# Strassen scheme: the second product a quarter unit later, casts in 2 KB rows, one quadrant cast by ScalarE, w_in's split stored

## The chip, the cores and the metric

The kernel runs on one core of a Trainium2 chip. The metric is the device time of one execution in microseconds, as the median of several runs. Beside it there is one profiled execution, whose trace gives each instruction with its start, its length and what it waited for.

## The reference

Two stages follow each other. Channel attention over 4 batches of 6080 tokens with 256 channels, then a feed-forward layer over all 24320 tokens with 2048 hidden channels:

```python
def _attn_ref(q, k, v, tau):                    # q, k, v: (4, 6080, 256) float32
    qn = q / (np.linalg.norm(q, axis=1, keepdims=True) + 1e-06)
    kn = k / (np.linalg.norm(k, axis=1, keepdims=True) + 1e-06)
    s = kn.transpose(0, 2, 1) @ qn / tau        # (4, 256, 256)
    a = np.exp(s - s.max(-1, keepdims=True))
    a /= a.sum(-1, keepdims=True) + 1e-09
    return v @ a

def _moe_ref(x, w_in, w_out):                   # x: (24320, 256), w_in: (256, 2048), w_out: (2048, 256)
    h = x @ w_in
    g = np.where(h > 0.0, h, np.exp(np.minimum(h, 0.0)) - 1.0)
    return g @ w_out
```

## The kernel before

**What is multiplied.** Attention's result is not formed: `a` is folded into the weights, so that the first product of a batch is `v` times (`a` times `w_in`), the second is `g @ w_out`. Each float32 operand is split into two parts, a high part rounded to TensorE's fast type (float32r) and a low part, the rest. A product is then three matmuls: high by high, high by low, low by high. "hi" and "lo" in names are these parts; a *cast* makes a high part, a subtraction on VectorE the low part.

**Stages.** The first 596 us hold batch 0 and the preparation of batch 1. Then comes the Strassen stage: batches 1 to 3 in 36 chunks of 512 or 496 tokens, each chunk in 4 *units* (`fq`, 512 hidden channels each), 144 units in all. Beside the units of batches 1 and 2 TensorE, and the others, compute the next batch's attention: 24 row groups of q and k each (gram matmuls, lines 203 and 210; squares for the norms), then the norms and the softmax, then the next weights (`plan_s`).

**A unit's first product.** The 2x2 blocks of weights and tokens are multiplied by the Strassen-Winograd scheme: seven `product` calls of six matmuls each (line 1102), into three PSUM banks. `A11 B11` goes into `bank_a`, `S3 T3` into `bank_e`; ScalarE copies them to `bank_b` and to the SBUF tile `p7`; `S2 T2`, `S1 T1` and `S4 B22` add into `bank_b`, `A12 B21` into `bank_a`, `A22 T4` into `bank_e`, and VectorE makes the sums between them (lines 1490 and 1498). The four quadrants of h then stand in `bank_a` (e11), `bank_b` (e12), `bank_e` (e21) and `p7` (e22). `relu_exp` (ScalarE, two instructions) and `largest` (VectorE) turn each into g, in the tile `held`.

**Splitting g.** `hi_part` casts one quadrant by a DMA that GpSimd issues (line 1186); `lo_parts` subtracts for a row of two quadrants (line 1189). Row 0 is e11 and e12 (tile `g1`), row 1 is e21 and e22 (`g2`). The last cast (e21) and both low parts are issued in the next unit: the cast behind `A11 B11`, row 0's low part ahead of VectorE's sum after `S2 T2`, row 1's behind that sum.

**The second product.** A unit gives eight *items* to the list `outs` (four 128-channel pieces of g by two halves of the output); an item is three matmuls (lines 1125 to 1127) into the accumulators `po`. `multiply_out(n, now)` takes n items off the list at fixed places between the products: 2, 1, 2, 1 and 2 a unit. With 6 items of the stage before and four empty entries at its head, the list runs 10 items behind: row 0's first item stands behind the next unit's `A12 B21`, and row 1's last two behind the second product of the unit after it.

**What sets the order.** On the five engines the order is the order in which Python issues instructions. The work for later batches is in queues of tasks, one per engine and level. A unit is 4 ticks; `spend(engine, budget, now)` takes tasks that are ready at tick `now` off an engine's queues, lower levels first, while their listed costs fit the budget. A task is ready when its `when` has come and each task that it depends on was issued at least `GAP` (or `late`) ticks ago. Between matmuls of the items, `beside` issues matmuls of the PE queue. A square (ScalarE, line 1287) writes the only buffer `sq`; GpSimd then issues a DMA that adds `sq` to `acc` (line 1290), and the next square waits until that has landed.

## Time and profile before

| | |
|---|---|
| median of 2 runs | 2329.24 us (2328.5 to 2329.99) |
| profiled execution | 2332.99 us, span 2331.2 us, mean granted TensorE clock 0.977 |
| busy share of the span | TensorE 94%, VectorE 69%, ScalarE 61%, GpSimd 27% |
| DMA | 345.47 MB; GpSimd's queue 38.9% of 16 engines, SyncE's 15.9% |
| the Strassen stage | begins 596 us after the span's start |

A row of a timeline gives the start in us from the span's start, the length in us, the engine, the line and operation, output<-inputs, and in brackets the idle time ahead of it with what ended it. A row of a group ends in busy us, mean ns of one, idle us before them and what ended most of that. A row of stretches gives for each engine the busy us with the number of instructions, then the granted TensorE clock as a share of full speed, the mean busy share of the DMA engines, and GB/s. A row of DMA issues gives the number, the size of one, and the median us from issue to landing. PE is TensorE, PEld its weight loads, DVE VectorE, ACT ScalarE, POOL GpSimd, SP SyncE.

### The profile page before, as it was taken

To read this page: it belongs to the slowest core of one execution; us is meant where nothing else is said; L and a number is where in the kernel's file an instruction comes from. 1 tells how busy PE (TensorE), PEld (TensorE's weight loads), DVE (VectorE), ACT (ScalarE), POOL (GpSimd) and SP (SyncE) were. 2 spreads that over 40 slices of the span, in tenths; PEclk is the share of its full clock that TensorE was granted. 3 is DMA by queue.
4 is the path that set the end of the run, shared out by engine and by line. 5 is a ranking of instruction groups with operands and counts; after the bars stand their busy time and mean duration, and the time that the engine had idled before them with its cause. 6 is when DMAs were issued, how large, how long until landed. Compare 5 with 4: busy or idle time off the path is not lost. (4 is left out here: it accounts for less than half of the span.)

```text
span 2331.2 us, 35484 instructions
## 1 busy us (share of the span) xinstructions
PE 2200.9 (94%) x12833; PEld 1967.5 (84%) x12833; DVE 1599.7 (69%) x2322; ACT 1419.1 (61%) x2380; POOL 633.4 (27%) x909
## 2 busy tenths in 40 slices
PE   9999999999898898899998898898899999999999
PEld 8888888998787777788997787787798889988988
DVE  7987777778665565567676666665677667767765
ACT  6877676677555455556565555555566566666665
POOL 0000000001333333332444333343334433333332
PEclk9999999999999999999999999999999999999999
DMA  9221222211577877675567777787557545555543
GB/s 338 93 87 36 79 64 73 66 40 50 148 194 183 208 194 179 174 178 143 152 162 212 198 200 203 183 202 188 147 147 187 152 125 150 138 146 131 144 126 108
DMA packets 264174, 345.47 MB, mean 148 GB/s; under 512 B 19776, under 2 KB 198976, under 8 KB 264000
## 3 DMA queue, kind: packets, MB, share of 16 engines
q0 software_dynamic: 201600, 224.17, 38.9%
q1 hardware_dynamic: 62256, 118.91, 15.9%
q8 instruction: 102, 1.67, 0.3%
q14 instruction: 72, 0.59, 0.1%
q10 hardware_dynamic: 144, 0.13, 0.0%
HBM read 134.33 MB, written 27.00 MB: 69 GB/s over the span
## 5 line engine op out<-in xcount | busy, mean ns | idle before, releaser
L1186 POOL DMA_DIRECT2D g<-held x576 | 409.8, 712 | 1061.1 <-issue 390.0
L1125 PE MATMUL po<-g,wo 128*128 128x512 f32 (+1 forms) x1158 | 453.1, 391 | 74.0 <-DMA g<-held 69.9
L1189 DVE TENSOR_TENSOR g<-held,g 128x1024 fp32r<-128x1024 f32 (+1 forms) x288 | 351.4, 1220 | 242.4 <-DMA g<-held 216.2
L1127 PE MATMUL po<-g,wo 128*128 128x512 f32 (+1 forms) x1158 | 455.8, 394 | 27.7 <-DVE g L1189 27.0
L1126 PE MATMUL po<-g,wo 128*128 128x512 f32 (+1 forms) x1158 | 447.2, 386 | 0.0
L1180 ACT ACTIVATE held<-held 128x512 f32<-128x512 f32 (+1 forms) x576 | 360.6, 626 | 18.3
L1125 PEld LDWEIGHTS po<-g,wo 128*128 128x128 f32 x1158 | 226.6, 196 | 96.3 <-issue 58.2
L1127 PEld LDWEIGHTS po<-g,wo 128*128 128x128 f32 x1158 | 225.4, 195 | 81.9 <-DVE g L1189 52.6
L1102 PEld LDWEIGHTS bank_b<-t,s 128*128 128x128 f32 x1728 | 238.6, 201 | 48.2 <-DVE bank_e L1490 33.6
L1102 PE MATMUL bank_b<-t,s 128*128 128x256 f32 (+1 forms) x1728 | 263.4, 291 | 11.1 <-ACT bank_b L1480 3.2
L1102 PE MATMUL bank_e<-t,s 128*128 128x256 f32 (+1 forms) x1728 | 241.6, 276 | 3.8 <-DVE held L1183 3.7
L1126 PEld LDWEIGHTS po<-g,wo 128*128 128x128 f32 x1158 | 226.7, 196 | 18.7
L1179 ACT ACTIVATE held<-bank_a 128x512 f32<-128x512 f32 (+1 forms) x144 | 84.8, 589 | 241.9 <-PE bank_a L1102 103.2
L1102 PEld LDWEIGHTS bank_e<-t,s 128*128 128x128 f32 x1728 | 217.0, 193 | 5.7 <-PE bank_a L1102 5.7
L1287 ACT ACTIVATE sq<-raw 128x1024 f32<-128x1024 f32 x46 | 48.8, 1060 | 218.0 <-DMA acc<-sq 212.2
L1102 PE MATMUL bank_a<-s,s 128*128 128x256 f32 (+1 forms) x1296 | 179.6, 275 | 0.0
L1102 PEld LDWEIGHTS bank_a<-s,s 128*128 128x128 f32 x1296 | 170.1, 192 | 5.3
L115 DVE TENSOR_TENSOR g<-e,g 128x512 fp32r<-128x512 f32 (+1 forms) x192 | 131.8, 686 | 48.3 <-ACT g L114 46.9
L114 ACT CAST g<-e 128x512 fp32r<-128x512 f32 (+1 forms) x192 | 116.7, 608 | 69.6 <-DVE e L445 37.6
L1183 DVE SCALAR_TENSOR_TENSOR held<-held,bank_a 128x512 f32<-128x512 f32 (+1 forms) x144 | 97.1, 674 | 85.7 <-ACT held L1180 85.7
L1480 ACT COPY bank_b<-bank_a 128x512 f32<-128x512 f32 (+1 forms) x144 | 81.6, 566 | 111.4 <-PE bank_a L1102 89.2
L1179 ACT ACTIVATE held<-p 128x512 f32<-128x512 f32 (+1 forms) x144 | 89.7, 623 | 91.3 <-DVE p L1498 91.3
(221 smaller groups left out, 4266.7 us busy)
## 6 DMA issues: line engine op xcount, KB each, us to landing
g<-held POOLq DMA_DIRECT2D x384, 256.0 KB, 2.5
g<-held POOLq DMA_DIRECT2D x192, 248.0 KB, 2.5
acc<-sq POOLq DMA_DIRECT2D x46, 512.0 KB, 6.6
raw<-in_q_dram SPq DMA_DIRECT2D x76, 256.0 KB, 3.5
raw<-in_k_dram SPq DMA_DIRECT2D x76, 256.0 KB, 4.2
v<-in_v_dram SPq DMA_DIRECT2D x32, 512.0 KB, 4.2
out_dram<-o SPq DMA_DIRECT2D x56, 256.0 KB, 2.7
qk<-in_q_dram POOLq DMA_DIRECT2D x46, 256.0 KB, 6.6
```

Source lines behind the costliest of these rows:

```text
L114: nc.scalar.copy(hi, src)
L115: nc.vector.tensor_sub(lo, src, hi.bitcast(F32))
L1102: nc.tensor.matmul(bank[:, j, 0:hn], w[:, x, js], y, start=(begin and j == 0 and k == 0), stop=(j == 1 and k == 2), skip_group_check=True,)
L1125: yield nc.tensor.matmul(o, wo[:, f, 0, ds], hi, start=begin, stop=False)
L1126: yield nc.tensor.matmul(o, wo[:, f, 1, ds], hi, start=False, stop=False)
L1127: yield nc.tensor.matmul(o, wo[:, f, 0, ds], lo, start=False, stop=end)
L1179: nc.scalar.activation(e, h, AF.Relu, scale=-1.0)
L1180: nc.scalar.activation(e, e, AF.Exp, scale=-1.0)
L1183: nc.vector.scalar_tensor_tensor(e, e, -1.0, h, op0=ALU.add, op1=ALU.max)
L1186: nc.gpsimd.dma_start(g[:, 0, :, half, 0:hn], e)
L1189: nc.vector.tensor_sub(g[:, 1].rearrange("p j r t -> p (j r) t")[:, :, 0:hn], held[:, x].rearrange("p j r t -> p (j r) t")[:, :, 0:hn], g[ ...
L1480: nc.scalar.copy(vb, va)
```

## The change

- The list `outs` gets six empty entries in place of four, and the places of its items become 2 behind `S3 T3`, 2 behind `A12 B21`, 2 behind `S1 T1`, 2 behind `A22 T4`. The two token halves of an output half follow each other.
- The high parts of g get fixed tiles, one for even and one for odd units, the low parts a third; a quadrant is one row of 2 KB per partition (512 elements) where it was two of 1 KB. Row 1 of odd units is held in two tiles of its own (`others`), and its low part is two subtractions. The weights' tiles (`s_tiles`) are laid out the same way, high parts together.
- e12 is cast by ScalarE, right behind the four quadrants' `relu_exp`.
- Row 0's low part stays ahead of the sum behind `S2 T2`; row 1's goes behind `A22 T4`.
- Batch 1 stores the two parts of `w_in` in DRAM (`wi_scr`); batches 2 and 3 load them by one DMA a quarter, without a load, a cast and two subtractions.
- Square, accumulate and other tasks get other levels, delays (`late`) and budgets; the sum of the two rows of `acc` (`fold_sum`) goes from GpSimd to VectorE; row groups are spread over 30 units (`PACE`) by their due times where it was 24.

The diff, cut to its core:

```diff
     w_scr = dram.tile([FQ, P, KT, CH], F32, name="w_scr")
+    wi_scr = dram.tile([FQ, P, 2, KT, CH], F32, name="wi_scr")
...
         split(hl[:, 0], hl[:, 1], src)
+        nc.sync.dma_start(wi_scr[fq], hl.bitcast(F32))
...
-        s_tiles[fq] = work.tile([P, SPARE + 1, 2, HF], F32R, tag="wp", bufs=2 * KT, name=f"s_{fq}")
+        s_tiles[fq] = work.tile([P, 2, SPARE + 1, HF], F32R, tag="wp", bufs=2 * KT, name=f"s_{fq}")
...
-                gap = 0 if d.engine == self.engine else max(GAP[self.engine], self.late)
+                gap = 0 if d.engine == self.engine else GAP[self.engine] if self.late is None else self.late
...
-                if not able or able[0].cost > budget:
+                if not able or able[0].cost > budget + 0.3:
...
-            task(ACT, 0.6, lambda: copy_out(c, dt), level=0)
+            task(ACT, 0.6, lambda: copy_out(c, dt), level=-1)
...
-    outs += [None] * 4
+    outs += [None] * 6
...
-    held = work.tile([P, 2, 2, 2, HF], F32, tag="qk", bufs=3, name="held")
+    held = work.tile([P, 2, 2, 2 * HF], F32, tag="qk", bufs=3, name="held")
+    others = [work.tile([P, 2 * HF], F32, tag="e", bufs=3, name=f"other_{x}") for x in range(2)]
+    parts_of_g = []
...
-    def hi_part(g, half, e, hn):
-        nc.gpsimd.dma_start(g[:, 0, :, half, 0:hn], e)
...
+    def part_of_g(u, row, x):
+        k = 1 if x else 2 * (u % 2)
+        if len(parts_of_g) == k:
+            parts_of_g.append(work.tile([P, 2, 2, 2 * HF], F32R, tag="g", bufs=3, name=f"g_{k}"))
+        return parts_of_g[k][:, row]
+
+    def hi_part(u, row, half, hn, by_act=False):
+        to, e = part_of_g(u, row, 0)[:, half, 0 : 2 * hn], exact(u, row, half, hn)
+        if by_act:
+            nc.scalar.copy(to, e)
+        else:
+            nc.gpsimd.dma_start(to, e)
+
+    def lo_parts(u, row, hn):
+        hi, lo = (part_of_g(u, row, x)[:, :, 0 : 2 * hn] for x in range(2))
+        if row == 1 and u % 2 == 1:
+            for half in range(2):
+                nc.vector.tensor_sub(lo[:, half], exact(u, row, half, hn), hi[:, half].bitcast(F32))
+        else:
+            nc.vector.tensor_sub(lo, held[:, row, :, 0 : 2 * hn], hi.bitcast(F32))
...
-                nc.gpsimd.dma_start(state[b, "wi", fq][:, 0], w_scr[fq])
...
-            wis = [task(DVE, 0.685, lambda jt=jt: wi_lo(jt), [x, y], level=2, late=2) for jt in range(KT)]
+                nc.gpsimd.dma_start(state[b, "wi", fq], wi_scr[fq])
...
-    PACE = PERIOD * 24 / NG
+    PACE = PERIOD * 30 / NG
...
-            s = task(ACT, 1.05, square, [x, *(acc_done if g else [prior.get("pw")])], when=t + 2, level=3)
+            s = task(ACT, 1.05, square, [x, *(acc_done if g else [prior.get("pw")])], when=t + 2, level=2, late=3 if g else 0)
             if g > 0:
-                acc_done = [task(POOL, 0.55, add, [s], level=2)]
+                acc_done = [task(POOL, 0.55, add, [s], level=1, late=1)]
...
-            nc.gpsimd.tensor_add(acc[:, :, 0, :], acc[:, :, 0, :], acc[:, :, 1, :])
+            nc.vector.tensor_add(acc[:, :, 0, :], acc[:, :, 0, :], acc[:, :, 1, :])
...
         multiply_out(2, now)
         spend(POOL, 3.9, now)
-        spend(ACT, 2.2, now)
-        spend(DVE, 2.8, now)
+        spend(ACT, 2.0, now)
+        spend(DVE, 2.4 if u % (FQ * NB) in (0, *range(FQ * NB - FQ, FQ * NB)) else 1.7, now)
+        product(bank_b, c, fq, "S2", "T2")
         if before is not None:
             before[1]()
-        product(bank_b, c, fq, "S2", "T2")
         nc.vector.tensor_add(ve, vb, vp)
+        product(bank_a, c, fq, "A12", "B21")
+        relu_exp(e11, va)
+        multiply_out(2, now)
+        spend(ACT, 0.7, now + 1)
+        product(bank_b, c, fq, "S1", "T1")
+        nc.vector.tensor_add(vp, vb, vp)
+        multiply_out(2, now + 1)
+        largest(e11, va)
+        hi_part(u, 0, 0, hn)
+        spend(POOL, 1.2, now + 1)
+        product(bank_b, c, fq, "S4", "B22")
+        product(bank_e, c, fq, "A22", "T4")
         if before is not None:
             before[2]()
-        product(bank_a, c, fq, "A12", "B21")
-        relu_exp(e11, va)
-        spend(POOL, 0.6, now + 1)
-        multiply_out(1, now)
-        product(bank_b, c, fq, "S1", "T1")
-        nc.vector.tensor_add(vp, vb, vp)
-        largest(e11, va)
...
-        hi_part(g1, 1, e12, hn)
+        hi_part(u, 0, 1, hn, True)
         multiply_out(2, now + 2)
+        spend(DVE, 1.4, now + 2)
+        spend(ACT, 0.4, now + 2)
+        spend(POOL, 3.3, now + 2)
+        spend(SP, 1, now + 2)
...
-        for y, g in ((2, g1), (0, g2)):
-            for j in range(2):
-                for dt in range(DT):
-                    outs.append((c, 4 * fq + y + j, (g, j), dt))
+        for y, row in ((2, 0), (0, 1)):
+            for dt in range(DT):
+                for j in range(2):
+                    outs.append((c, 4 * fq + y + j, ((u, row), j), dt))
```

Where this moves instructions, the built programs show, engine by engine.

TensorE, from `S2 T2` to `S1 T1` of the 100th unit, before and after (`g1` is row 0, `g2` row 1; after the change `g_0` and `g_2` are the high parts of even and odd units, `g_1` the low parts):

```order
L1102 MATMUL bank_b_5084<-t_0_4714,s_3_5088 128x256 x6
L1102 MATMUL bank_a_16045<-s_1_4869,s_3_5088 128x256 x6
L1125 MATMUL po_36_0_15890<-g1_16004,wo_83 128x512
L1126 MATMUL po_36_0_15890<-g1_16004,wo_83 128x512
L1127 MATMUL po_36_0_15890<-g1_16004,wo_83 128x512
L1102 MATMUL bank_b_5084<-t_0_4714,s_3_5088 128x256 x6
```
```order
L1104 MATMUL bank_b_5089<-t_0_4716,s_3_5095 128x256 x6
L1104 MATMUL bank_a_15868<-s_1_4873,s_3_5095 128x256 x6
L1127 MATMUL po_36_1_15760<-g_2_5249,wo_83 128x512
L1128 MATMUL po_36_1_15760<-g_2_5249,wo_83 128x512
L1129 MATMUL po_36_1_15760<-g_1_5223,wo_83 128x512
L1127 MATMUL po_36_1_15760<-g_2_5249,wo_83 128x512
L1128 MATMUL po_36_1_15760<-g_2_5249,wo_83 128x512
L1129 MATMUL po_36_1_15760<-g_1_5223,wo_83 128x512
L1104 MATMUL bank_b_5089<-t_0_4716,s_3_5095 128x256 x6
```

Before, the first item of the previous unit's row 0 stands between them; now the last two items of the unit before that do, and row 0 begins behind `S1 T1`.

GpSimd, in units of batch 1 with a row group beside them, before and after (casts write `g`, the accumulate `acc`, the casts of the next row group `qk`):

```order
L1186 DMA g1_7371<-held_5086 128x2x256
L1186 DMA g2_7399<-held_5086 128x2x256
L1186 DMA g1_7371<-held_5086 128x2x256
L1186 DMA g2_7399<-held_5086 128x2x256
L1290 DMA acc_2_5211<-sq_7338 128x1024
L1306 DMA qk_7449<-in_q_dram 128x512
L1306 DMA qk_7449<-in_k_dram 128x512
```
```order
L1204 DMA g_0_5162<-held_5091 128x512
L1298 DMA acc_2_5213<-sq_7528 128x1024
L1204 DMA g_0_5162<-held_5091 128x512
L1314 DMA qk_7604<-in_q_dram 128x512
L1314 DMA qk_7604<-in_k_dram 128x512
L1204 DMA g_0_5162<-held_5091 128x512
```

Four casts and then the accumulate have become three casts (e11, e22, e21), with the accumulate behind the first and the row group's casts behind the second.

ScalarE, at the boundary of two units of batch 1, before and after (`held<-bank_b` is e12's `relu_exp`, `held<-bank_e` e21's):

```order
L1179 ACTIVATE held_5086<-bank_b_5084 128x2x256
L1180 ACTIVATE held_5086<-held_5086 128x2x256
L1179 ACTIVATE held_5086<-bank_e_7753 128x2x256
L1180 ACTIVATE held_5086<-held_5086 128x2x256
L1480 COPY bank_b_5084<-bank_a_7866 128x512
L1482 COPY p7_5087<-bank_e_7867 128x512
```
```order
L1183 ACTIVATE held_5091<-bank_b_5089 128x512
L1184 ACTIVATE held_5091<-held_5091 128x512
L1183 ACTIVATE held_5091<-bank_e_7273 128x512
L1184 ACTIVATE held_5091<-held_5091 128x512
L1202 CAST g_0_5162<-held_5091 128x512
L1490 COPY bank_b_5089<-bank_a_7381 128x512
L1492 COPY p7_5094<-bank_e_7382 128x512
```

The cast of e12 now stands between e21 and the copy into `bank_b`.

More of the change, by code (lines that the diff above doesn't have):

```diff
@@ L947, in channel_attention_then_elu_ffn @@
     ACT, DVE, POOL, PE, SP = "act", "dve", "pool", "pe", "sp"
-    queues = {(e, level): [] for e in (ACT, DVE, POOL, PE, SP) for level in range(4)}
+    queues = {(e, level): [] for e in (ACT, DVE, POOL, PE, SP) for level in range(-2, 4)}
     GAP = {ACT: 0, DVE: 0, POOL: 2, PE: 2, SP: 0}
@@ L964, in ready, with task @@
             return True
-    def task(engine, cost, fn, deps=(), when=0, level=1, late=0):
+    def task(engine, cost, fn, deps=(), when=0, level=1, late=None):
         t = Task(fn, tuple(d for d in deps if d is not None), when)
@@ L974, in spend @@
     def spend(engine, budget, now):
-        for level in range(4):
+        for level in range(-2, 4):
             queue = queues[engine, level]
@@ L1312, in plan_rows @@
             h = task(*((POOL, 1.1) if n == 2 else (ACT, 1.05)), hi, before if n == 2 else [x, *before], when=t + PACE * g, level=2)
-            los = [task(DVE, 0.685, lambda y=y, lo=lo: lo(y), [h, x], level=2, late=2 if n == 2 else 0) for y in range(2)]
+            los = [task(DVE, 0.685, lambda y=y, lo=lo: lo(y), [h, x], level=2, late=4 if n == 2 else None) for y in range(2)]
             mine = [s, *los]
@@ L1344, in fold_lo @@
             nc.vector.tensor_sub(parts[:, 1], state[b, "acc"][:, :, 0, :], parts[:, 0].bitcast(F32))
-        f = task(POOL, 1.19, fold_sum, adds, level=1)
-        f = task(ACT, 0.61, fold_hi, [f], level=1)
-        folded = task(DVE, 0.685, fold_lo, [f], level=1)
+        f = task(DVE, 0.685, fold_sum, adds, level=0, late=4)
+        f = task(ACT, 0.61, fold_hi, [f], level=0)
+        folded = task(DVE, 0.685, fold_lo, [f], level=0)
         def row_copy(ct):
@@ L1470, in channel_attention_then_elu_ffn @@
         assert (b, fq) in s_ready, (b, fq, u)
-        e11, e12, e21, e22 = (held[:, x, :, half, 0:hn] for x, half in ((0, 0), (0, 1), (1, 0), (1, 1)))
+        e11, e12, e21, e22 = (
+            exact(u, row, half, hn).rearrange("p (j t) -> p j t", j=2) for row in range(2) for half in range(2)
+        )
         vp = p7[:, :, 0:hn]
```

90 lines of the change are left out of this document (35 added, 55 removed).

## The prediction

> **What bounds the kernel now.** I read the page's head first, then busy time by stage, then the waits, then one bad unit in the timeline. TensorE carries the span.
>
> ```profile
> span 2331.2 us, 35484 instructions
> PE 2200.9 (94%) x12833; PEld 1967.5 (84%) x12833; DVE 1599.7 (69%) x2322; ACT 1419.1 (61%) x2380; POOL 633.4 (27%) x909
> ```
>
> No other engine is near its limit, so what can be won is TensorE's 130 us of idle time and what the idling does to its clock. Where does it idle? The next fence holds three stretches of the Strassen stage twice, first all instructions and then those of line 1102 alone (columns: stretch, length, PE busy, PEld busy, then in the first three DVE, ACT and POOL busy; granted clock; DMA share; GB/s). A unit issues 42 matmuls on line 1102, so the count divided by 42 is the number of units.
>
> ```profile
> 596.00:1082.00 486.00, 427.46 (x2562) 378.21 (x2561) 294.15 (x425) 257.59 (x432) 167.25 (x245) 0.94 0.72 183
> 1215.00:1689.00 474.00, 425.21 (x2573) 375.75 (x2572) 297.29 (x427) 256.87 (x429) 178.28 (x255) 0.96 0.75 191
> 1823.00:2278.00 455.00, 445.50 (x2902) 406.26 (x2901) 319.50 (x448) 284.01 (x485) 155.51 (x221) 0.99 0.53 139
> ...
> 596.00:1082.00 486.00, 206.01 (x1512) 195.77 (x1512) 0.94 0.72 183
> 1215.00:1689.00 474.00, 202.80 (x1511) 192.64 (x1510) 0.96 0.75 191
> 1823.00:2278.00 455.00, 237.94 (x1846) 232.84 (x1845) 0.99 0.53 139
> ```
>
> The two **loaded** stretches, where the next batch's gram runs beside the units, hold 36 units each at 13.5 and 13.2 us; the **light** one holds 44 at 10.35 us. The TensorE timeline gives what a unit must take: from one A11·B11 product to the next, undisturbed, 9.87 us, a product 0.67 us. It also gives the price of the gram: two items of the second product take 1.29 us alone (804.43 to 805.72) and 2.28 us with six gram matmuls between them (807.71 to 809.99), so eight of them, one row group, cost 1.32 us.
>
> ```profile
> 2003.82 0.83 PE L1102 MATMUL bank_a<-s,s 128*128 128x256 f32 x6
> 2004.48 0.83 PE L1102 MATMUL bank_e<-t,s 128*128 128x256 f32 x6
> ...
> 2013.69 0.83 PE L1102 MATMUL bank_a<-s,s 128*128 128x256 f32 x6
> ...
> 804.43 0.38 PE L1125 MATMUL po<-g,wo 128*128 128x512 f32 x1
> ...
> 805.72 0.38 PE L1125 MATMUL po<-g,wo 128*128 128x512 f32 x1
> ...
> 807.71 0.38 PE L1125 MATMUL po<-g,wo 128*128 128x512 f32 x1
> ...
> 809.99 0.83 PE L1102 MATMUL bank_b<-t,s 128*128 128x256 f32 x6
> ```
>
> A loaded stretch therefore needs 36 x 9.87 + 24 x 1.32 = 387 us; it takes 486 and 474, so **99 + 87 = 186 us are lost** there. The light one needs 44 x 9.87 = 434 and takes 455: 21 us, 0.48 us a unit. The waits name the cause, and one loaded unit shows the order of events (columns of the first four: who waited for whom, us in total, times, longest).
>
> ```profile
> DVE g L1189 <- DMA g<-held: 216.2, 112, 6.2
> ACT sq L1287 <- DMA acc<-sq: 212.2, 29, 10.1
> PE po L1125 <- DMA g<-held: 69.9, 33, 4.6
> PE po L1127 <- DVE g L1189: 27.0, 43, 3.0
> ```
> ```profile
> 803.11 1.06 ACT L1287 ACTIVATE sq<-raw 128x1024 f32<-128x1024 f32 x1 [5.55 <-DMA acc<-sq]
> 804.08 0.58 ACT L1179 ACTIVATE held<-bank_a 128x512 f32<-128x512 f32 x1
> ...
> 809.08 1.46 POOL L1186 DMA_DIRECT2D g<-held  x2 [0.21 <-issue]
> 810.53 0.94 POOL L1290 DMA_DIRECT2D acc<-sq  x1
> ...
> 815.98 1.22 DVE L1189 TENSOR_TENSOR g<-held,g 128x1024 fp32r<-128x1024 f32 x1 [6.12 <-DMA g<-held]
> ...
> 815.99 0.45 PE L1125 MATMUL po<-g,wo 128*128 128x512 f32 x1 [4.50 <-DMA g<-held]
> ...
> 817.25 0.80 PE L1127 MATMUL po<-g,wo 128*128 128x512 f32 x1
> 817.86 1.65 PE L1102 MATMUL bank_b<-t,s 128*128 128x256 f32 x6
> 819.30 0.62 PE L1125 MATMUL po<-g,wo 128*128 128x512 f32 x1
> ```
>
> ScalarE stands 5.55 us before a square, because the accumulating DMA that reads `sq` has not landed. The four quadrants behind it come out late and together; GpSimd issues the last two casts at 809.08 and the next accumulate right behind. The last cast lands at 816: VectorE's low part has stood 6.12 us for it, TensorE 4.50. Then, from 815.99 to 819.30, come eleven matmuls (four of a full 512 columns at 0.22 us, one gram matmul at 0.11, a product at 0.67) that need 1.64 us; they take 3.31. The clock is cut, which is the granted 0.94 and 0.96 above (0.06 x 486 + 0.04 x 474 = 48 us of the 186).
>
> **The change, part by part.** The prices:
>
> ```profile
> L1189 DVE TENSOR_TENSOR g<-held,g 128x1024 fp32r<-128x1024 f32 (+1 forms) x288 | 351.4, 1220 | 242.4 <-DMA g<-held 216.2
> L115 DVE TENSOR_TENSOR g<-e,g 128x512 fp32r<-128x512 f32 (+1 forms) x192 | 131.8, 686 | 48.3 <-ACT g L114 46.9
> L114 ACT CAST g<-e 128x512 fp32r<-128x512 f32 (+1 forms) x192 | 116.7, 608 | 69.6 <-DVE e L445 37.6
> ...
> g<-held POOLq DMA_DIRECT2D x384, 256.0 KB, 2.5
> ...
> acc<-sq POOLq DMA_DIRECT2D x46, 512.0 KB, 6.6
> ...
> w_scr<-wf SPq DMA_DIRECT2D x4, 512.0 KB, 2.9
> ```
> ```profile
> q0 software_dynamic: 201600, 224.17, 38.9%
> q1 hardware_dynamic: 62256, 118.91, 15.9%
> ```
>
> *A quarter unit later.* Two of a unit's eight items, 1.29 us, move behind their product, and row 1's four items move past the next unit's first two products: 2 x 0.67 + 1.29 = 2.6 us more for casts and low parts. The mean wait of TensorE for a cast is 69.9 / 33 = 2.1 us, so this alone covers the usual wait, not the longest of 4.6. VectorE still writes row 0's low part ahead of the sum that frees `bank_b` for S1·T1, but two items instead of one stand before that product, 0.65 us more room, and VectorE's side work there has a budget of 1.7 in place of 2.8. Row 1's low part goes from ahead of S1·T1 to behind A22·T4; behind it wait two quadrants' maxima (below, the slower rival).
>
> *The accumulate and the square.* In the old order the square stands right behind the accumulate's issue and pays its landing, 212.2 / 29 = 7.3 us at a time. In the new one the accumulate is issued behind the first quadrant's cast, about 9.3 us into an 11.2 us unit (an estimate from the product and item lengths above), and the next square comes 1.9 us into the next unit, behind the two copies of A11·B11 and S3·T3, that is at 13.1. Landing 6.6 us after its issue, it makes ScalarE wait 9.3 + 6.6 - 13.1 = 2.8 us. Square done 5.6 us into the unit, against 5.0 at which the first quadrant's sum is ready: 0.6 us late, and the second quadrant isn't ready before 8. So this wait is hidden; it costs from landings of about 9 us on.
>
> *One quadrant on ScalarE.* 144 x 608 ns = 88 us more ScalarE work (1419 becomes 1507 us, 65%) and 144 of 576 casts fewer on GpSimd's queue. What stands behind the cast is the copy into `bank_b`, for which the next product waits. In a light unit ScalarE idles there:
>
> ```profile
> 2003.18 0.63 ACT L1180 ACTIVATE held<-held 128x512 f32<-128x512 f32 x1
> 2004.68 0.57 ACT L1480 COPY bank_b<-bank_a 128x512 f32<-128x512 f32 x1 [0.88 <-PE bank_a L1102]
> ```
>
> 0.88 us of idle time covers 0.61: cost nothing, and at most (no cover) 88 us.
>
> *2 KB rows.* No row of the page prices the old cast against the new one, only two queues: 38.9% of 16 engines for 201600 packets is 72 ns for a mean of 1.1 KB, 15.9% for 62256 is 95 ns for 1.9 KB. So half as many packets of twice the size cost about two thirds: the casts' share of the DMA engines falls, by the quarter that leaves and by this. Landing 2.5 us gains between 0 and 0.4 us; I take 0. The Trainium skill ("DMA: Bandwidth & Descriptors", sections "Specifications" and "Anatomy of one DMA — SWDGE (gpsimd) path") speaks against this part: rows of 512 B and more already move at line rate, and a GpSimd DMA costs about 2.0 us plus its bytes at 436 GB/s. That makes 2.6 us for 256 KB whatever the rows (an estimate from that page; the trace has 2.5). By it the rows gain nothing, the DMA engines are relieved only by the quarter that leaves, and the time would stand nearer to the upper end below, about 2178.
>
> *w_in's split stored.* Four stores of 1 MB in batch 1: 0 to 4 x 2 x 2.9 = 23 us if something waited for them; nothing but a buffer two uses later does, so 0. Sixteen low parts of 686 ns go from VectorE (11 us); splitting one low part in two on every second unit gives back 72 x (2 x 686 - 1220) = 11 us. VectorE has 31% idle: 0.
>
> **The sum.** Lost in the loaded stretches: 186. Left there afterwards: between 0 and what a light unit loses now, 0.48; I take half, 0.24 x 72 = 17 us, because a part of the light stretch's loss is itself a wait for low parts, which now come earlier than they are needed (that stretch alone, columns as above):
>
> ```profile
> PE po L1127 <- DVE g L1189: 5.4, 6, 2.3
> ```
>
> The light stretch also loses half of its 21. Gain 186 - 17 + 10 = 179 us; the span becomes 2152. The profiled execution took 2332.99 against a median of 2329.24, so 1.8 us lie around its span and the median is 3.7 lower: 2152 + 1.8 - 3.7 = **2150 us**. With nothing left over it is 2122, with 0.48 us a unit left and no gain elsewhere 2178.
>
> **The rivals.** *Half of it stays* (0.14). The accumulate now sits between the casts of one unit, so the second and third cast queue behind its 512 KB; the DMA engines are 72 to 75% busy in the loaded stretches, and shorter units raise that. If half of the 186 us stay: 2331 - 93 - 5 - 2 = 2231. The 38.9% share speaks for it, the 2.6 us of new distance against it. The Trainium skill ("TensorE: Matmul & The Clock Gate", section "Part 1: The HAM clock gate") has the clock halved only after about 3.4 us of idling. By that rule halved waits would not cut the clock at all, and this case would give back the 24 us that I leave in it for the clock: about 2207. The trace agrees so far as it shows the cut behind a gap of 4.50 us.
>
> *The change doesn't do what it says* (0.08): with landings near the 10.1 us that the longest wait shows, ScalarE still stands 9.3 + 10.1 - 13.1 = 6.3 us before a square and remains the pacemaker, and the bunch of late casts only moves with it. A quarter of the 186 us at most, for the quarter unit, is then won, or nothing: 2283 to 2330. Against it stands the median landing of 6.6.
>
> *Slower* (0.04): VectorE's low part of row 1 now stands between two quadrants' maxima, and ScalarE's cast, with the `bank_b` copy behind it, waits for the second of them. The last cast is issued some 1.9 us into the next unit and its low part's turn comes at 8.6. If it lands later than those 6.7 us (casts land in 2.5, the accumulate that may stand ahead in 6.6), the chain VectorE, ScalarE, TensorE stalls in each unit with a row group. It decides from a mean stall of 3.3 us in 54 such units (three of four loaded ones), which eats the 179 us; at 4.7 us, 3 of waiting and the 1.67 that the cut clock cost above, it is 254 us: 2150 + 254 = 2404.
>
> **Chances.** Forecast 0.70, below it (the floor of 2122 is itself a sum of modelled lengths) 0.04. The range 2112 to 2240 takes in the forecast's ends and the half case. A measurement of this kernel can tell about 2% from no change, 2283 to 2376: faster 0.88, within 0.08, slower 0.04.
>
> **What would show it.** The wait of ScalarE's square for the accumulate falls from 212 us below 100, VectorE's for casts from 216 below 60, TensorE's for casts from 70 below 15; the granted clock of the loaded stretches rises to 0.98 or more and their units go from 13.3 to about 11 us. GpSimd's cast count is 432. I am wrong if TensorE still idles more than 60 us after 596, or if `bank_b` products wait for ScalarE.

## The result, and the profile after

The changed kernel takes **2147.41 us** (median of 2 runs, 2145.76 to 2149.07) against 2329.24: a ratio of 0.9219, 95% interval 0.918 to 0.9259. The forecast was 2150. The page's head, its queue row and the landings of the changed kernel:

```profile
span 2147.3 us, 34893 instructions
PE 2114.3 (98%) x12833; PEld 1934.9 (90%) x12833; DVE 1587.0 (74%) x2380; ACT 1485.0 (69%) x2524; POOL 439.8 (20%) x763
...
q0 software_dynamic: 101376, 191.00, 32.6%
...
g<-held POOLq DMA_DIRECT2D x192, 256.0 KB, 2.3
g<-other POOLq DMA_DIRECT2D x96, 256.0 KB, 4.2
acc<-sq POOLq DMA_DIRECT2D x46, 512.0 KB, 4.7
```

TensorE is idle for 33 us of the span instead of 130. The stretches of the Strassen stage, cut at the first product of a unit: the two loaded ones of 36 units, and 47 units of the light one; below, the last alone with line 1104, the product's line now.

```profile
596.88:994.65 397.77, 389.00 (x2557) 360.21 (x2556) 288.03 (x436) 277.90 (x466) 119.79 (x209) 0.99 0.74 200
1127.27:1524.07 396.80, 390.37 (x2576) 362.37 (x2575) 291.98 (x441) 276.82 (x465) 123.49 (x212) 1.00 0.74 201
...
1657.60:2126.20 468.60, 251.72 (x1974) 248.67 (x1974) 1.00 0.38 115
```

The loaded stretches went from 486 and 474 to 398 and 397 us, 11.05 and 11.02 us a unit: 165 of the span's 184 us come from there. The last 47 units, all light, took 484.6 us before (from 1822.58 to 2307.21) and take 468.6 now, 16 us less or 9.97 us a unit instead of 10.31. The clock that was cut to 0.94 and 0.96 is back at 0.99 and 1.00. The waits that answer to those of before (who waited for whom, us in total, times, longest):

```profile
PE bank_b L1104 <- DVE bank_e L1500: 18.6, 32, 1.5
PE gram L203 <- DVE qk L1318: 4.6, 2, 2.3
PE bank_b L1104 <- ACT bank_b L1490: 3.3, 3, 2.0
...
DVE g L1212 <- DMA g<-held: 24.2, 18, 3.4
...
DVE g L1210 <- DMA g<-other: 7.2, 7, 1.9
...
ACT sq L1295 <- DMA acc<-sq: 19.9, 19, 2.3
```

VectorE's waits for casts of g are two rows now, 31 us together. TensorE no longer waits for a cast at all, and the waits for low parts of g (27.0 us before) are gone too. One loaded unit, which begins at 785.25, and a square of the next:

```profile
785.25 0.83 PE L1104 MATMUL bank_a<-s,s 128*128 128x256 f32 x6
...
785.92 0.54 POOL L1204 DMA_DIRECT2D g<-held  x1 [0.17 <-issue]
...
792.92 1.22 DVE L1212 TENSOR_TENSOR g<-held,g 128x1024 fp32r<-128x1024 f32 x1
...
795.25 0.92 POOL L1298 DMA_DIRECT2D acc<-sq  x1
...
800.18 1.06 ACT L1295 ACTIVATE sq<-raw 128x1024 f32<-128x1024 f32 x1 [1.55 <-DMA acc<-sq]
```

The last cast of a unit (e21, 785.92) has 7.0 us until row 1's low part is due at 792.92, which begins without a wait. The accumulate is issued 10.0 us into the unit and has landed when the next square begins 4.93 us later; ScalarE stood 1.55 us.

### The profile page after: what moved, and what is told of

It reads as the page before. It is cut to its first block, busy times and chain, and to the rows that moved or that the text cites. A ratio compares the mean times of both kernels' runs of the same rounds, so it can differ in the third digit from the quotient of the medians.

```text
span 2147.3 us, 34893 instructions
## 1 busy us (share of the span) xinstructions
PE 2114.3 (98%) x12833; PEld 1934.9 (90%) x12833; DVE 1587.0 (74%) x2380; ACT 1485.0 (69%) x2524; POOL 439.8 (20%) x763
## 3 DMA queue, kind: packets, MB, share of 16 engines
q0 software_dynamic: 101376, 191.00, 32.6%
## 5 line engine op out<-in xcount | busy, mean ns | idle before, releaser
L1127 PE MATMUL po<-g,wo 128*128 128x512 f32 (+1 forms) x1158 | 439.5, 380 | 0.0
L1128 PE MATMUL po<-g,wo 128*128 128x512 f32 (+1 forms) x1158 | 437.7, 378 | 0.0
L1129 PE MATMUL po<-g,wo 128*128 128x512 f32 (+1 forms) x1158 | 437.7, 378 | 0.0
L1204 POOL DMA_DIRECT2D g<-held x288 | 154.0, 535 | 946.6 <-DVE held L1187 612.3
L1212 DVE TENSOR_TENSOR g<-held,g 128x1024 fp32r<-128x1024 f32 (+1 forms) x216 | 264.0, 1222 | 24.9 <-DMA g<-held 24.2
L1184 ACT ACTIVATE held<-held 128x512 f32<-128x512 f32 (+1 forms) x432 | 270.4, 626 | 13.8
L1104 PEld LDWEIGHTS bank_b<-t,s 128*128 128x128 f32 x1728 | 233.6, 192 | 50.3 <-DVE bank_e L1500 33.6
L1506 DVE TENSOR_TENSOR p<-bank_b,p 128x512 f32<-128x512 f32 (+1 forms) x144 | 98.8, 686 | 232.8 <-PE bank_b L1104 232.8
L1104 PE MATMUL bank_b<-t,s 128*128 128x256 f32 (+1 forms) x1728 | 244.4, 278 | 22.2 <-DVE bank_e L1500 18.6
L1129 PEld LDWEIGHTS po<-g,wo 128*128 128x128 f32 x1158 | 219.3, 189 | 28.4
L1128 PEld LDWEIGHTS po<-g,wo 128*128 128x128 f32 x1158 | 220.8, 191 | 17.3
L1127 PEld LDWEIGHTS po<-g,wo 128*128 128x128 f32 x1158 | 221.1, 191 | 13.4
L474 PE MATMUL po<-g,wo 128*128 128x512 f32 (+1 forms) x378 | 142.7, 377 | 0.0
L472 PE MATMUL po<-g,wo 128*128 128x512 f32 (+1 forms) x378 | 142.6, 377 | 0.0
L470 PE MATMUL po<-g,wo 128*128 128x512 f32 (+1 forms) x378 | 142.6, 377 | 0.0
```

Source lines behind the costliest of these rows:

```text
L470: nc.tensor.matmul(o, wo[:, f, 0, ds], hi, start=first(c, f), stop=False)
L472: nc.tensor.matmul(o, wo[:, f, 1, ds], hi, start=False, stop=False)
L474: nc.tensor.matmul(o, wo[:, f, 0, ds], lo, start=False, stop=last(c, f))
L1104: nc.tensor.matmul(bank[:, j, 0:hn], w[:, x, js], y, start=(begin and j == 0 and k == 0), stop=(j == 1 and k == 2), skip_group_check=True,)
L1127: yield nc.tensor.matmul(o, wo[:, f, 0, ds], hi, start=begin, stop=False)
L1128: yield nc.tensor.matmul(o, wo[:, f, 1, ds], hi, start=False, stop=False)
```

## The experiments

Two questions: which part of the change brought the 182 us, and are the parts worth the same by themselves? Each part was undone in the changed kernel, and the two strongest were put alone into the kernel of before.

**The quarter unit undone, e1_lag.** The order of the items and the low parts' places stay as changed.

```diff
-    outs += [None] * 6
+    outs += [None] * 4
-        spend(DVE, 2.4 if u % (FQ * NB) in (0, *range(FQ * NB - FQ, FQ * NB)) else 1.7, now)
+        spend(DVE, 2.4 if u % (FQ * NB) in (0, *range(FQ * NB - 3 * FQ, FQ * NB)) else 1.7, now)
```

> The changed kernel with four empty entries in place of six, so the second product a quarter unit earlier; VectorE's larger budget is given to eight more units of each batch. Theory A: with the accumulate out of the way the casts land 2.3 us after their issue and well ahead of their use; TensorE waits for casts and low parts stay under 30 us, 2150 to 2180. Rival B: the quarter unit was what covered the waits, so most of the loss comes back: 2220 or more.

2431.57 us, ratio 1.0449 (1.0432 to 1.0465): within rival B's "2220 or more", but slower than before, which neither side said. Two waits appear that neither the kernel of before nor the changed one has:

```profile
PE po L1129 <- DVE g L1212: 228.3, 48, 10.4
...
DVE tt L1028 <- DMA v<-in_v_dram: 220.3, 30, 11.5
```

Row 1's low part is issued behind `A22 T4`, and with the list two items earlier TensorE wants its product right behind `A22 T4` too. VectorE itself stands before that for a chunk's load of v. Which of the two set the time isn't separated, so this run says only that the six entries and row 1's low part go together.

**The old order of square and accumulate, e2_square.**

```diff
-            s = task(ACT, 1.05, square, [...], when=t + 2, level=2, late=3 if g else 0)
+            s = task(ACT, 1.05, square, [...], when=t + 2, level=3, late=0)
-                acc_done = [task(POOL, 0.55, add, [s], level=1, late=1)]
+                acc_done = [task(POOL, 0.55, add, [s], level=2, late=4)]
```

> The changed kernel with the old order of the accumulate alone: the accumulating DMA is issued one unit after its square, and the next square stands right behind it on ScalarE. Theory A (ScalarE's blocked square was the head of the chain): ScalarE again stands 4.7 us or more before each of 46 squares (some 200 us in all), the quadrants come late and together, and even with the later second product much comes back: 60 to 150 us, so 2205 to 2300. Rival B (what mattered was the distance between the casts and their use: the quarter unit, the cast on ScalarE, the longer rows): ScalarE waits just as long, but TensorE doesn't; 2147 to 2165.

2272.28 us, ratio 0.9765 (0.9747 to 0.9782): 125 us lost. The wait is back at the size that it had before, with a wait of TensorE behind it:

```profile
ACT sq L1295 <- DMA acc<-sq: 208.0, 32, 9.5
...
PE bank_e L1104 <- DVE held L1187: 38.8, 17, 4.2
```

**e12 cast by a DMA again, e3_e12_dma.**

```diff
-        hi_part(u, 0, 1, hn, True)
+        hi_part(u, 0, 1, hn)
```

> The changed kernel with quadrant e12 cast by a DMA on GpSimd's queue again, issued at the unit's end. Theory A: the low part of row 0 then waits for that DMA, about 2 to 4 us after its issue, ahead of the sum that frees bank_b: VectorE's wait for casts goes from 24 us to 100 or more, TensorE's for VectorE from 19 to 40 to 100, 2165 to 2230. Rival: ScalarE's extra 88 us were a cost, and the time falls by up to 10 us.

2250.91 us, ratio 0.9671 (0.9649 to 0.9692): 103 us lost, for the reason that theory A gives and by more than its 2165 to 2230.

```profile
DVE g L1212 <- DMA g<-held: 195.8, 103, 5.4
...
PE bank_b L1104 <- DVE bank_e L1500: 97.6, 72, 3.2
```

Row 0's low part waits for the fourth cast DMA again; the sum into `bank_e` is queued behind it on VectorE, and `S1 T1` waits for that sum.

**1 KB rows, e4_1kb.** The casts write two rows of 1 KB per partition; the low parts and the second product read them so.

```diff
-        to, e = part_of_g(u, row, 0)[:, half, 0 : 2 * hn], exact(u, row, half, hn)
+        to = part_of_g(u, row, 0).rearrange("p j (r t) -> p j r t", r=2)[:, :, half, 0:hn]
+        e = exact(u, row, half, hn).rearrange("p (j t) -> p j t", j=2)
```

> The changed kernel with the high and low parts of g laid out as before, two rows of 1 KB per partition for each cast in place of one of 2 KB; nothing else moves. Theory (rows by the measured queues): the casts' load on the DMA engines rises by half, GpSimd's queue from 32.6% to about 36%; landings rise from 2.25 to 2.5 us, in the loaded stretches more; 0 to 15 us slower, 2147 to 2162. Rival (bytes alone count): landing 2.25 us and time unchanged within 3 us.

2151.05 us, ratio 0.9237 (0.9219 to 0.9255), against 0.9219 (0.918 to 0.9259) for the changed kernel: no difference that these intervals tell. Queue and landings:

```profile
q0 software_dynamic: 156672, 191.00, 36.2%
...
g<-held POOLq DMA_DIRECT2D x192, 256.0 KB, 2.6
```

Longer rows save 3.6 points of the DMA engines' time. The two medians of a landing, 2.6 and 2.3 us, overstate the difference: e8, with 2 KB rows, has 2.6 too. Between 1700 and 2100 us, where neither accumulates nor row groups are issued, the casts land in 2.5 us with 1 KB rows and in 2.2 to 2.3 with 2 KB. VectorE waits 46 us for casts instead of 31; TensorE waits for none in either kernel.

**The quarter unit undone with all that belongs to it, e5_clean_lag.** Row 1's low part goes back behind VectorE's sum into `bank_e`, and `dt` runs inside `j` again. As in e1, VectorE's larger allowance holds in eight more units of a batch.

```diff
-    outs += [None] * 6
+    outs += [None] * 4
-        spend(DVE, 2.4 if u % (FQ * NB) in (0, *range(FQ * NB - FQ, FQ * NB)) else 1.7, now)
+        spend(DVE, 2.4 if u % (FQ * NB) in (0, *range(FQ * NB - 3 * FQ, FQ * NB)) else 1.7, now)
         nc.vector.tensor_add(ve, vb, vp)
+        if before is not None:
+            before[2]()
...
-        if before is not None:
-            before[2]()
```

> The changed kernel with the quarter unit alone undone, cleaner than in the run before: four empty places in the list of the second product, its items in the old order (the two halves inside), and the low part of a unit's second row back right behind VectorE's sum into bank_e. VectorE's larger allowance (2.4 us) is given to the last 12 units of a batch instead of the last 4, so that the operands still come in time; everything else stays as changed. Theory A (the quarter unit buys room for the casts, and one chunk's v load behind an output store made the earlier run of it as slow as it was): 2200 to 2300 us, VectorE's low parts waiting 60 to 250 us in all for casts, and no large wait for v. Rival B (the earlier 2432 us is the price of the quarter unit itself): 2400 us or more. Rival C (with the square and the quadrant cast in their new places the quarter unit isn't needed): 2140 to 2165 us.

2252.49 us, ratio 0.9657 (0.9632 to 0.9683): 105 us lost, as theory A said. The allowance is not the cause of most of it: by the lengths of the units, the eight units that got it lose 12 and 11 us in the two batches, the first 32 units of each batch 45 and 44. One of the bad units:

```profile
814.92 0.91 POOL L1298 DMA_DIRECT2D acc<-sq  x1
...
816.01 0.90 POOL L1314 DMA_DIRECT2D qk<-in_q_dram  x1
816.53 0.92 POOL L1314 DMA_DIRECT2D qk<-in_k_dram  x1
817.37 0.60 POOL L1204 DMA_DIRECT2D g<-other  x1
...
824.42 1.29 DVE L1210 TENSOR_TENSOR g<-other,g 128x512 fp32r<-128x512 f32 x2 [4.40 <-DMA g<-other]
...
826.37 1.17 PE L1104 MATMUL bank_b<-s 128*128 128x256 f32 x6 [3.81 <-DVE p L1508]
...
828.62 0.63 PE L1127 MATMUL po<-g,wo 128*128 128x512 f32 x1
```

Behind the accumulate and two casts of the next row group, e21's cast (817.37) takes 7.0 us to land. Row 1's low part waits for it, the sum into `p7` stands behind the low part, and `S4 B22` waits for the sum. After the gap of 3.81 us two products take 2.25 us where they take 1.34.

**The order of square and accumulate alone in the kernel of before, e6_before_acc_order.** The tasks get the changed kernel's levels and delays, and GpSimd's allowance behind `A12 B21` is 1.2 instead of 0.6.

```diff
-            s = task(ACT, 1.05, square, [...], when=t + 2, level=3)
+            s = task(ACT, 1.05, square, [...], when=t + 2, level=2, late=3 if g else 0)
-                acc_done = [task(POOL, 0.55, add, [s], level=2)]
+                acc_done = [task(POOL, 0.55, add, [s], level=1, late=1)]
```

> The kernel of before with one part of the change alone: the square and its accumulate DMA get the changed kernel's priorities and places, all else as before. If the parts add up, it gains what its undoing cost (125 us): 2204 us, 2175 to 2235. Theory A (each of the parts takes away one of several waits that stand in the same units, so one alone leaves the others to set the unit): 2250 to 2325 us, ScalarE's wait for the accumulate under 60 us instead of 212, and VectorE's wait for casts still 150 us or more. Rival: no gain at all, 2320 to 2340, if the waits for the square lay wholly beside those for the casts.

2213.30 us, ratio 0.9483 (0.9455 to 0.9511): 119 us gained, what undoing it cost. Theory A, that one part alone would leave most of the loss, fell.

```profile
DVE g L1189 <- DMA g<-held: 166.8, 97, 4.5
...
ACT sq L1287 <- DMA acc<-sq: 4.7, 4, 2.2
```

The square's wait is gone although the accumulate still lands 6.3 us after its issue. VectorE still waits three quarters as long for casts as before (166.8 of 216.2 us), but TensorE's own wait for them fell from 69.9 to 12.8 us: most of that wait went with ScalarE's.

**e12 on ScalarE alone in the kernel of before, e7_before_e12_act.**

```diff
-        hi_part(g1, 1, e12, hn)
+        nc.scalar.copy(g1[:, 0, :, 1, 0:hn], e12)
```

> The kernel of before with one part of the change alone: the cast of the quadrant e12 is done by ScalarE instead of a DMA that GpSimd issues. If the parts add up, it gains what its undoing cost (103 us): 2226 us, 2195 to 2250. Theory A (several waits in the same units, one alone leaves the others): 2270 to 2330 us, VectorE's wait for casts down from 216 to 130 to 200 us and ScalarE's wait for the accumulate still about 200. Rival: slower than before, 2335 to 2360, because ScalarE, which waits for the accumulate, now also delays this cast.

2279.00 us, ratio 0.9773 (0.9754 to 0.9792): 54 us gained, half of what its undoing cost. VectorE's wait for casts fell further than expected, and a new one of TensorE took its place, behind the square's, which stays:

```profile
DVE g L1189 <- DMA g<-held: 78.5, 37, 5.7
...
ACT sq L1287 <- DMA acc<-sq: 201.0, 29, 9.3
...
PE bank_b L1102 <- DVE p L1498: 52.7, 21, 4.8
```

**Both in the kernel of before, e9_before_two.** The edits of the two runs above together; their core:

```diff
-            s = task(ACT, 1.05, square, [...], when=t + 2, level=3)
+            s = task(ACT, 1.05, square, [...], when=t + 2, level=2, late=3 if g else 0)
-        hi_part(g1, 1, e12, hn)
+        nc.scalar.copy(g1[:, 0, :, 1, 0:hn], e12)
```

> The kernel of before with two parts of the change together: the order of the square and its accumulate DMA, and ScalarE's cast of e12; the second product's place, the buffers and w_in's load as before. Each alone gained 119 and 54 us. Theory A (the two together and the quarter unit are each needed for the rest; without the quarter unit the changed kernel took 2252 us): 2200 to 2255 us, little below the 2213 us of the accumulate order alone, VectorE's wait for casts at 80 to 170 us. Rival B (the gains add): 2157 us, 2140 to 2180, and the quarter unit is worth no more than 10 us on top of the two. Rival C (the ScalarE cast delays the square's chain): above 2255 us.

2174.56 us, ratio 0.9334 (0.9321 to 0.9348): 155 of 182 us, near the sum of 119 and 54. Rival B's time held, but not its 10 us for the quarter unit: the quarter unit, the rows, w_in's split and all else together are worth 27 us on top. Budgets, `PACE` and the moved `fold_sum` were not tried by themselves, nor was the quarter unit alone in the kernel of before. TensorE's wait for casts and ScalarE's for the accumulate are gone without them. What stays is TensorE's wait for low parts, as long as before (27.0 us), which the changed kernel is rid of:

```profile
ACT sq L1287 <- DMA acc<-sq: 4.3, 4, 2.7
...
PE po L1127 <- DVE g L1189: 26.7, 19, 3.2
...
PE po L1125 <- DMA g<-held: 0.4, 1, 0.4
```

Why does the old place of the second product do well here and cost 105 us in e5? GpSimd's order differs:

```profile
816.87 0.71 POOL L1186 DMA_DIRECT2D g<-held  x1 [1.13 <-DVE held L1183]
...
818.13 0.56 POOL L1306 DMA_DIRECT2D qk<-in_q_dram  x1
...
820.33 1.22 DVE L1189 TENSOR_TENSOR g<-held,g 128x1024 fp32r<-128x1024 f32 x1
```

Here a unit's last cast (816.87) goes ahead of the side work, and row 1's low part (820.33) finds it landed. In the changed kernel the allowance of 3.3 us at a unit's end puts the row group's casts ahead of e21's cast; e5 shows what that costs without the quarter unit. Whether this order is the whole of the difference between 105 and 27 us wasn't tried.

**The low part of t later, e8_t_low_later.** In light units of the changed kernel every fourth one loses half a microsecond. VectorE there, ahead of row 0's low part, which follows at 1762.38:

```profile
1761.78 0.69 DVE L1040 TENSOR_TENSOR t<-tt,t 128x512 fp32r<-128x512 f32 x1 [0.82 <-ACT t L1035]
```
```diff
-                task(DVE, 0.685, lambda k=k: t_lo(d, k), [y], when=t + PERIOD, level=-1)
+                task(DVE, 0.685, lambda k=k: t_lo(d, k), [y], when=t + PERIOD, level=-1, late=1)
```

> The changed kernel with one edit: the low part of a chunk's t operands on VectorE may come only in a later allowance than the cast on ScalarE that it needs, so it no longer stands, waiting, ahead of the low part of row 0 and the sum into bank_e. In the trace of the changed kernel every fourth unit of the unloaded stretch lasts 10.41 us instead of 9.87, with VectorE waiting 0.82 us for that cast. Theory A (that wait is what the unit loses): 24 such units times 0.54 us = 13 us less, 2134 us (2130 to 2141). Rival B (the unit is bound by something beside it, or the later low part stalls the e21 casts as much): 2144 to 2152 us. Rival C (pushed later, it makes the operands of the next chunk late): above 2155 us.

2145.01 us, ratio 0.9198 (0.918 to 0.9215). The unit that lasted from 1758.56 to 1768.97 now lasts 9.87 us, like its neighbours:

```profile
1757.49 0.83 PE L1104 MATMUL bank_a<-s 128*128 128x256 f32 x6
...
1767.36 0.83 PE L1104 MATMUL bank_a<-s,s 128*128 128x256 f32 x6
```

The time is in rival B's range, and theory A's wait is real: its count was wrong. Only the light units show it, twelve of the 24; the 47 of them take 463.1 us instead of 468.6. The two loaded batches take 531.0 and 530.2 us, as long as without the edit (530.4 and 530.3), probably because their gram matmuls set the pace; no run shows that. The median's 2.4 us is inside the intervals.

**Row groups apart as well, e11_groups_apart.**

```diff
-            before = ... if g >= 2 else [prior.get("lo" if g else "lo before")]
+            before = ... if g >= 2 else [prior.get("lo" if g else "lo before"), *(los if g else ())]
```

> The kernel of the run e8_t_low_later with one more edit: the cast DMAs of a batch's second group of rows (g = 1) wait for the low parts of its first group, so GpSimd no longer issues four of these DMAs one behind the other ahead of a quadrant's cast. In the changed kernel units 6 and 54 last 15.6 and 15.3 us instead of 11.2, VectorE waiting 3.4 us for that quadrant's cast and the gram matmul 2.3 us for a low part. Theory A (the bunch is the cause): 2 x 4.3 = 8.6 us less than e8_t_low_later, so 2136 us (2131 to 2141). Rival B (the later groups of the batch now lie later and the bunch comes elsewhere, at the batch's end): 2141 to 2155 us. Rival C (the softmax of the batch comes late): above 2160 us.

2140.97 us, ratio 0.9189 (0.9174 to 0.9205), span 2136.4. Units 6 and 54 went from 15.6 and 15.3 us to 11.2; TensorE's 4.6 us of waiting for `qk` is gone. Another unit near the end of a batch grew from 12.6 to 16.2, as rival B said, so that 4 us of theory A's 8.6 came; the time lies where the two ranges meet. This is the fastest kernel of the study. The intervals don't tell it from the changed kernel.

**w_in's old load, e10_w_in_old.**

```diff
-                nc.gpsimd.dma_start(state[b, "wi", fq], wi_scr[fq])
-            wi = task(POOL, 0.6, load, ...)
+                nc.sync.dma_start(src, w_scr[fq])
+            y = task(POOL, 0.55, wi_hi, ...)
+            wis = [task(DVE, 0.685, lambda jt=jt: wi_lo(jt), [x, y], level=2, late=2) for jt in range(KT)]
-        spend(DVE, 2.4 if u % (FQ * NB) in (0, *range(FQ * NB - FQ, FQ * NB)) else 1.7, now)
+        spend(DVE, 2.4 if u % (FQ * NB) in (0, *range(FQ * NB - 4 * FQ, FQ * NB)) else 1.7, now)
```

> The changed kernel with the load of w_in alone undone: a batch's w_in comes unsplit by SyncE, is cast by a DMA, and VectorE makes the low part (2 instructions for each of 4 tiles and batch), and VectorE's larger allowance of 2.4 us holds in the last 16 units of a batch instead of 4, so that these come in time. Theory A (8 instructions of 0.69 us and a load of 4 x 512 KB for a batch, beside an idle VectorE): 2140 to 2160 us. Rival B (VectorE's softmax stretch is full, TensorE waits in it): 2165 to 2190 us, the loss within the 12 units before each batch ends.

2174.62 us, ratio 0.9335 (0.932 to 0.9351): 27 us lost. The time is rival B's; the place is not quite. 26 us are lost in the last 16 units beside a batch, 18 of them in the first four of these, ahead of rival B's twelve. VectorE and TensorE in the worst unit, which begins at 967.0, and in the next:

```profile
975.78 0.69 DVE L1248 TENSOR_TENSOR wi<-wraw,wi 128x512 fp32r<-128x512 f32 x1 [4.24 <-DMA wi<-w_scr]
...
978.22 1.64 PE L1103 MATMUL bank_b<-t,s 128*128 128x248 f32 x6 [5.82 <-DVE bank_e L1510]
...
989.90 1.79 DVE L1405 RECIPROCAL ry<-ry 128x130 f32<-128x130 f32 x2
...
993.97 0.93 PE L1103 MATMUL bank_b<-t,s 128*128 128x248 f32 x6 [2.87 <-DVE bank_e L1510]
```

In the worst unit a low part of w_in stands on VectorE, waiting 4.24 us for its cast to land, ahead of row 0's low part and the sum behind it, and TensorE waits 5.82 us for that sum. The same happens in the next batch (1.91 and 3.49 us, at 1517.26 and 1519.70). These two units, 18.6 and 16.9 us against 11.4, make 12.6 of the 27 us. In the unit that begins at 985.7 it is the norms' chain: with the allowance of 2.4 us more of it gets in ahead of row 0's low part, and TensorE waits 2.87 us. How much of the rest is the low parts of w_in and how much the allowance that they need, no run separates.

**Row 1's low part alone moved back, e12_row1_place.** The second product stays a quarter unit later. All units' low parts share one tile; so in this kernel the last two of row 1's items read the low part of the unit after theirs.

```diff
         nc.vector.tensor_add(ve, vb, vp)
+        if before is not None:
+            before[2]()
...
-        if before is not None:
-            before[2]()
```

> The changed kernel with the low part of a unit's second row alone moved back, from behind A22 T4 to right behind VectorE's sum into bank_e; the second product stays a quarter unit later. In the run e5_clean_lag, which undid both, VectorE stood 4.40 us at that low part for the cast of e21, which lay behind an accumulate and two casts of q and k, and TensorE's S4 B22 waited 3.81 us for the sum behind it. Theory A (what the quarter unit is worth is that it lets this low part stand later): as slow as e5_clean_lag, 2225 to 2270 us, with S4 B22 waiting 40 to 100 us in all for VectorE. Rival B (the second product's own place is what counts): 2140 to 2170 us. Rival C (each is half): 2180 to 2215.

2591.03 us, ratio 1.1129 (1.1109 to 1.1148), far outside all three.

```profile
PE po L1129 <- DVE g L1210: 182.4, 71, 5.9
PE po L1129 <- DVE g L1212: 152.8, 71, 6.5
```

TensorE waits 142 times in 144 units for a low part. The run doesn't price the place; it shows, from the other side than e1, that the place and the six entries are one edit.

## Why the prediction was right, and where it was not

- **The bound and the sum.** TensorE's idle time and its cut clock in the loaded stretches were what could be won. The sum took 169 us from them; 165 came. For the light units it took 10; 16 came, and what remains (4.7 us) is nearly all the wait that e8 removes. That the two misses cancel is luck.
- **The square.** Forecast: issue at 9.3 us, 2.8 us of waiting. The unit above has 10.0 and 1.55; over all 46 squares it is 19.9 us, 0.43 each. The forecast took a landing of 6.6 us, and it is 4.7 now. That was not needed: in e6 it is 6.3, with 4.7 us of waiting in all. The rival with a pacemaking square is out.
- **Half of it stays.** Casts do queue behind the accumulate, as that rival said (see the last section), but the unit above leaves a cast 7.0 us, and VectorE's waits for casts are 31 us in all.
- **The quarter unit.** The prediction made it the cover for casts ("this alone covers the usual wait"). The step that failed is what the other parts leave for it: with the old place of the second product, e9 has 0.4 us of TensorE waiting for casts. There the quarter unit can still remove the waits for low parts, 26.7 us; on top of the two other parts it and all else are worth 27 us. Inside the changed kernel, whose GpSimd order leans on it, it is worth 105.
- **e12 on ScalarE.** "Cost nothing" was right: `bank_b` products wait 3.3 us for ScalarE's copy, three times, where they waited 3.2 us before, four times. (By the letter the last sign of being wrong came true, since it named no size.) It was also too little: the step priced only ScalarE's 88 us. A cast that no longer passes GpSimd's queue and a DMA's landing is worth 54 us alone and 103 in the changed kernel, because on VectorE row 0's low part stands ahead of the sum that frees a bank.
- **2 KB rows.** Taken as 0, between 0 and 0.4 us of a landing: where nothing disturbs the casts it is 0.2 to 0.3, and there is no difference in the time that the intervals tell. The prediction's "two thirds" was too much. Two packets of 72 ns against one of 95 would save 49 ns; between e4 and the changed kernel the queue's share of 16 engines falls by 1257 us for 55296 packets fewer, 23 ns each. The Trainium skill ("DMA: Bandwidth & Descriptors", section "Specifications") has rows from 512 B on at line rate; the traces disagree in the queue's share, 36.2% for 1 KB rows and 32.6% for 2 KB at the same bytes, and agree in what the kernel gains.
- **w_in stored.** Taken as 0 because "VectorE has 31% idle". That step failed: it priced the low parts by their length, and what costs is where they stand. In e10 one of them waits 4.24 us for its cast ahead of the sum that TensorE needs, and the old load with the allowance that it needs costs 27 us.
- **Slower.** It needed row 1's last cast to land later than its low part's turn at 8.6 us of a unit. In the unit above the turn came at 7.7 and without a wait, and VectorE's waits for all casts of g are 31 us. The place itself was a hazard, though: e1 is what happens when the second product doesn't move with it.
- **The clock.** It came back with the waits, as forecast. The rival's other price, 2207 us, rests on a limit that these traces don't bear out. The Trainium skill ("TensorE: Matmul & The Clock Gate", section "Part 1: The HAM clock gate") has the clock halved after about 3.4 us of idling; here it is halved behind gaps of 4.50 us (before) and 3.81 (e5), but also behind one of 2.28 us in the changed kernel (last section). Halving the wait of 4.50 would not have made the clock safe.

## What to carry to other kernels

Ask of each transfer what is queued behind the instruction that waits for it: in e6 the accumulate's landing hardly changed, its place did, and that was 119 of 182 us. Price a moved cast by the queues that it leaves, not only by the engine that it enters, and an instruction on a half idle engine by the wait that it may hold there, not only by its length. And test a part from both sides: three undone parts cost 125, 103 and 105 us, 333 of a gain of 182, while added to the old kernel two of them gave 155 together. The finished kernel leans on each of its parts.

## What was not expected of the hardware

The landing of a GpSimd DMA depends on what is issued around it more than on its own rows. The same 256 KB casts of `other` land in a median of 4.2 us in the changed kernel and in 2.3 in e2; there it is the accumulate, issued behind them, that takes 7.4 us instead of 4.7:

```profile
g<-other POOLq DMA_DIRECT2D x96, 256.0 KB, 2.3
...
acc<-sq POOLq DMA_DIRECT2D x46, 512.0 KB, 7.4
```

Counted over all 144 casts of `other`, the short ones too, 48 have an accumulate issued less than 4 us ahead of them in the changed kernel, and none has in e2. A row group's cast stands less than 3 us ahead of 14 of them in both.

The clock is cut in steps, and by shorter gaps than those of 4.50 and 3.81 us. In the changed kernel it stands at 0.5 three times before the kernel's last microsecond, for 3.41 us each, from 610.97, 665.58 and 1194.65 on; these starts are whole multiples of 3.41 us apart. The stretch ahead of the second cut, and the cut (columns as in the stretches above):

```profile
662.17:665.58 3.41, 1.13 (x6) 0.53 (x5) 3.41 (x6) 1.37 (x3) 0.55 (x1) 1.00 0.65 147
665.58:668.99 3.41, 3.41 (x11) 2.87 (x12) 2.83 (x4) 2.24 (x4) 1.06 (x2) 0.50 0.85 260
```

TensorE was idle for 2.28 us of the first row, waiting for a low part of `qk`. Laid on such a grid of 3.41 us, the Strassen stages of all 14 traces agree: behind a step at the whole clock in which TensorE was idle for more than 2.0 us the clock was always cut, behind one with less than 1.5 us never, and in between both occur (idle time by the modelled ends of the matmuls). So one gap can count or not by where it falls. Of two gaps of 2.87 us in e10, the one that ends at 993.97 lies across two steps, with 1.97 us in the first, and the clock stays at 1.00; the one that ends at 1536.04 has 2.62 us in one step, and the clock is 0.5 from 1535.79 on.
